# Top-k attention and a low-rank mixer on one core: first batch searched without folding and masked by GpSimd, second batch masked by the gap on both heads

## The chip, the cores and the metric

The kernel runs on one core of a Trainium2 chip. The metric is the device time of one execution in microseconds, as the median of several runs. The engines are PE (TensorE, matmuls), ACT (ScalarE), DVE (VectorE), POOL (GpSimd) and SP (SyncE, which issues the transfers here). Each works through its own stream of instructions in a fixed order; semaphores make one wait for another.

## The reference

Attention keeps, in each row of scores, the 32 largest, and then a block mixes over the sequence and over the channels. Everything is float32.

```python
B, H, S, D = q.shape                      # 8, 8, 576, 64
scores = scale * np.matmul(q, k.transpose(0, 1, 3, 2))
kth = np.partition(scores, -top_k, axis=-1)[..., -top_k:-top_k + 1]   # top_k = 32
mask = scores >= kth
scores = np.where(mask, scores, -1000000000.0)
attn = softmax(scores); attn_out = np.matmul(attn, v)
x = attn_out.transpose(0, 2, 1, 3).reshape(B, S, H * D)               # 8, 576, 512
h = x.transpose(0, 2, 1) @ U @ V                                      # rank 32
u = x + h.transpose(0, 2, 1)
out = u + np.maximum(u @ w_ch1, 0.0) @ w_ch2                          # 512 -> 2048 -> 512
```

(The softmax is written out in the original: the maximum is subtracted, and 1e-9 is added to the sum.)

## The kernel before

**Tiles and steps.** The 8 batches of 8 heads are 32 groups `g` of two heads (`NP`), four groups (`NPAIR`) a batch. The 576 query rows of a group are cut into four chunks of 128 rows with both heads (`t` = 0 to 3) and a last one (`t` = `NT` = 4), in which the remaining 64 rows of both heads share the 128 partitions. A pair (g, t) is a step `n = 5 g + t`; there are 160. Steps 0 to 19 are the first batch (`ALONE` = 20), 20 to 39 the second. From step 30 on (`ROUNDED`), for t below 4, `shared(g, t)` is true: there DVE and transfers turn the weights round rather than PE.

**One step.** `scores` makes S2, the tile Ssb of 128 x 2 x 576 scores, with PE and ACT copies. `front` searches each row's 32nd largest value with DVE: four times MAX8 (eight largest), with MATCH_REPLACE8 between them. It is a generator, advanced at several places of the main loop, and so spreads a step's work over its own and the following step.

**Folding.** Where a step has an entry in `folds`, each row's halves of 288 are folded: `pair` adds the halves as integers on POOL (L370, stage 0), takes their maximum on DVE (L372) and subtracts it from the sum on POOL (L373, stage 1), which leaves the smaller of each two. DVE searches the lower half with two MAX8 and one MATCH_REPLACE8 of 288 (L412, L414, L416), adds the 16 values found to the upper half, and does the four rounds on 304 elements instead of 576 (L426, L438, L443). Before, every step but (0, 0) is folded. `lower` has one buffer.

**Masking.** `ways(g, t)` says which heads are masked how. An "early" head gets its exponential on ACT within the search (L377, into a tile E), and DVE multiplies it by the mask and sums it (L446). A "gap" head gets, at the beginning of the next step, a very large number wherever a score lies below the 32nd (L461 and L464 on ACT), which POOL subtracts (L467), and then the exponential on ACT, which also sums (L377). Before, a two-head step outside `shared` masks head 1 early and head 0 by the gap; a shared one masks both by the gap and gives the exponential of head 1 a yield of its own (`ahead`). (3, 3) and (3, 4), the end of the first batch, have rules of their own.

**The rest.** `turns` transposes the weights with PE (L522, L527) and copies them with ACT (L523, L528); `values` multiplies by v (L556, L560, L546); `mixed` applies the low-rank mixer (L581 to L614); `mlp` is the large matmul part (L629, L648), which `fill` feeds in small portions as filler between the steps, by a fixed account (`share`, `due`). The filler begins when the first batch's attention is done. `next_params` loads the mixer's and the large part's weights and converts them: three ACT passes (L174, L175, L178), a shift on DVE (L186) and two integer additions on POOL (L187, L189), called a join below; this goes on until 326 us.

**Order.** The order on each engine is that in which the Python code issues instructions. In the first batch a step n runs: first MAX8 of step n; gap of step n - 1; scores and fold part one of n + 1; `values` of n - 3 and the `turns` of n - 2; second round of n; a join at t below 3; third round; exponential of n - 1; fold part two of n + 1; fourth round; a join at t = 0, 1 and 3; masking product of n. The first step whose DVE instructions come in a group is therefore L412, or L426 where nothing is folded.

Of the kernel before, what the change touches and what calls it, by code (L numbers as in the profile page):

```python
# [8 lines left out]
F32 = mybir.dt.float32  # L9
# [3 lines left out]
ALU = mybir.AluOpType  # L13

TOPK = 32
NEG = -3.0e38
# [10 lines left out]
def kernel(  # L27
# [28 lines left out]
    nc = tc.nc  # L56
    B, H, S, D = q.shape
    P = 128
# [4 lines left out]
    NT, TAIL = 4, 64  # L63
# [3 lines left out]
    NPAIR = H // 2  # L67
    NP = B * NPAIR

    CH = NT + 1  # L70
    ALONE = NPAIR * CH
# [11 lines left out]
    attn = ctx.enter_context(tc.tile_pool(name="attn", bufs=2))  # L83
# [265 lines left out]

    def fold(g, t):  # L350

        if 0 < g + t and g < NP:
            upper = attn.tile([P, 2, HALF + TOPK // 2], F32, tag="upper", name="upper")
            lower = attn.tile([P, 2, HALF], F32, tag="lower", name="lower", bufs=1)
            folds[g, t] = upper, lower
            pair(g, t, 0)
# [6 lines left out]
    def pair(g, t, stage):  # L363
        S2 = S2s[g, t]
        n = S2.shape[1]
        upper, lower = folds[g, t]
        top, bottom = upper[:, 0:n, 0:HALF], lower[:, 0:n].bitcast(U32)
        a, b = S2[:, :, 0:HALF], S2[:, :, HALF:S]
        if stage == 0:
            nc.gpsimd.tensor_tensor(bottom, a.bitcast(U32), b.bitcast(U32), ALU.add)  # L370
        else:
            nc.vector.tensor_tensor(top, a, b, ALU.max)  # L372
            nc.gpsimd.tensor_tensor(bottom, bottom, top.bitcast(U32), ALU.subtract)  # L373

    def weigh(chunk, E, nmax, total=None):

        nc.scalar.activation(E, chunk, AF.Exp, bias=nmax, scale=SCALE, accum_out=total)  # L377

    def ways(g, t):

        if (g, t) == (NPAIR - 1, NT - 1):
            return (0,), (1,)
        if (g, t) == (NPAIR - 1, NT):
            return (0,), ()
        if t == NT:
            return (), (0,)
        return ((), (1, 0)) if shared(g, t) else ((1,), (0,))

    def eased(g, t):
        return bool(ways(g, t)[1])  # L390

    def front(g, t):

        if t == 0:
            dens[g] = small.tile([P, 2 * NT + 1], F32, tag="den", name="den", bufs=3)
        S2, den = S2s.pop((g, t)), dens[g]
        n = S2.shape[1]  # L400
        chunks = [S2[:, c] for c in range(n)]
        sums = [den[:, 2 * t + c : 2 * t + c + 1] for c in range(n)]
        first = small.tile([P, 2, 8], F32, tag="first", name="first", bufs=3)
        nmax = small.tile([P, 2], F32, tag="nmax", name="nmax", bufs=4)
        order = (1, 0) if n == 2 else (0,)
        folded = (g, t) in folds
        if folded:
            upper, lower = folds.pop((g, t))
            curs = [upper[:, c] for c in range(n)]
            spots = [[upper[:, c, HALF + i : HALF + i + 8] for c in range(n)] for i in (0, 8)]  # L410
            for c in order:
                nc.vector.max(spots[0][c], lower[:, c])  # L412
            for c in order:
                nc.vector.match_replace(lower[:, c], spots[0][c], lower[:, c], NEG)  # L414
            for c in order:
                nc.vector.max(spots[1][c], lower[:, c])  # L416
        else:
            curs = list(chunks)
            places = [
                mlpp.tile([P, 2, WIDE], F32, tag="hT", name="hT", bufs=HT)  # L420
                .rearrange("p c n -> p (c n)")[:, 0:S]
                for _ in range(n)
            ]
        ms = [first[:, c] for c in range(n)]
        for c in order:
            nc.vector.max(ms[c], curs[c])  # L426
        yield
        early, gaps = ways(g, t)
        for i in range(1, TOPK // 8):
            if i == 1:  # L430
                nc.scalar.mul(nmax[:, 0:n], first[:, 0:n, 0], -SCALE)
                Es = {c: attn.tile([P, S], F32, tag="E", name="E") for c in early}
                for c in early:
                    weigh(chunks[c], Es[c], nmax[:, c : c + 1])
            for c in order:

                nxt = places[c] if i == 1 and not folded else curs[c]
                nc.vector.match_replace(nxt, ms[c], curs[c], NEG)  # L438
                curs[c] = nxt
            m8 = small.tile([P, 2, 8], F32, tag="m8", name="m8", bufs=4)  # L440
            ms = [m8[:, c] for c in range(n)]
            for c in order:
                nc.vector.max(ms[c], curs[c])  # L443
            yield
        for c in early:
            nc.vector.scalar_tensor_tensor(  # L446
                out=chunks[c],
                in0=chunks[c],
                scalar=ms[c][:, 7:8],
                in1=Es[c],  # L450
                op0=ALU.is_ge,
                op1=ALU.mult,
                accum_out=sums[c],
            )
        if t == NT:
            del qkTs[g]
        yield
        if gaps:
            lo, hi = min(gaps), max(gaps) + 1
            least = small.tile([P, 2], F32, tag="least", name="least", bufs=3)  # L460
            nc.scalar.mul(least[:, lo:hi], m8[:, lo:hi, 7], WIDEN)  # L461
            for c in gaps:
                gap = attn.tile([P, S], F32, tag="E", name="E")
                nc.scalar.activation(  # L464
                    gap, chunks[c], AF.Relu, bias=least[:, c : c + 1], scale=-WIDEN
                )
                nc.gpsimd.tensor_tensor(chunks[c], chunks[c], gap, ALU.subtract)  # L467
            yield
        ahead = order[0:1] if shared(g, t) else ()
        for c in ahead:  # L470
            weigh(chunks[c], chunks[c], nmax[:, c : c + 1], sums[c])
            yield
        for c in order:
            if c not in early and c not in ahead:
                weigh(chunks[c], chunks[c], nmax[:, c : c + 1], sums[c])
        if t == NT and g != NPAIR - 1:
            nc.scalar.activation(den, den, AF.Identity, bias=eps)
        yield

    def shared(g, t):  # L480


        return t < NT and g * CH + t >= ROUNDED
# [237 lines left out]
    def fill(k=1):  # L721


        nonlocal due
        for _ in range(k):
            if passes:
                passes.pop(0)()
            if mixing and next(mixing[0], True):
                mixing.pop(0)
            due += share * (SHORT if t == NT else 1) * (EARLY if n <= 2 * ALONE + 2 else 1)  # L730
            while due > 0:
                if not fillers:
                    due = 0.0
                    break
                done = next(fillers[0], None)
                if done is None:
                    fillers.pop(0)
                else:
                    due -= done
# [3 lines left out]
    t = 0  # L743
# [5 lines left out]
    for n in range(STEPS + 2):  # L749
        g, t = divmod(n, CH)  # L750
        if n < STEPS:
            if t == 0 and g + 1 < NP:
                load(g + 1)
            if t == 1 and g + 1 < NP:
                ready = prep(g + 1)
            fronts[n] = front(g, t)
            next(fronts[n])
        here, last = fronts.get(n, iter(())), fronts.pop(n - 1, iter(()))
        if n >= ALONE - 1 and n <= ALONE:

            if n < ALONE:
                next(last)
                values(*divmod(n - 3, CH))
                list(turning)
                next(here)
                next(last)
                scores(*divmod(n + 1, CH))
                fold(*divmod(n + 1, CH))
                values(*divmod(n - 2, CH))
# [11 lines left out]
            fill()  # L781
            scores(*divmod(n + 1, CH))
            fold(*divmod(n + 1, CH))
            next(here)
            while mixing:
# [9 lines left out]
            fill()  # L795
            continue
        ease = eased(*divmod(n - 1, CH))
        if n < ALONE:
            if ease:
# [26 lines left out]
        away = n <= STEPS and shared(*divmod(n - 1, CH))  # L826
# [6 lines left out]
        next(turning, None)  # L833
        fill()
        next(turning, None)
        if away:
            next(last)
        fill()
        next(turning, None)
        fill()  # L840
# [55 lines left out]
```

## Time and profile before

| | |
|---|---|
| median of 3 runs | 1759.32 us (1758.77 to 1759.58) |
| the profiled execution | 1761.93 us, of which the span of the profile is 1760.2 us |
| busy: PE, DVE, ACT, POOL | 1641.2, 1528.0, 1025.6, 965.7 us |
| fold, POOL L370 and L373 | x159 each, 218.3 and 204.3 us |
| gap subtraction, POOL L467, 128x576 | x263, mean 1410 ns |
| masking product, DVE L446, 128x576 | x25, 768 to 1668 ns, median 805 |
| maximum of a fold, DVE L372 | x159, mean 899 ns |
| MAX8 of 304 elements (L443) | x858, mean 464 ns |
| MAX8 and MATCH_REPLACE8 of 576 elements, first step | mean 744 and 740 ns |
| gap, ACT L464, 128x576 | x263, mean 769 ns |

A row of a timeline gives the start, the time, the engine, the line, the operation, output and inputs, and in brackets the idle time ahead of it with what ended it. Successive instructions of an engine overlap a little, so the distance from start to start is what one costs in a queue that is never empty: two paired MAX8 of 304 elements show 0.84 us together and start a new instruction 0.76 us later. Times of POOL rows are rougher than others.

### The profile page before, as it was taken

What the parts mean: (1) busy time and instruction counts of PE and PEld (TensorE: products, weight loads), DVE (VectorE), ACT (ScalarE), POOL (GpSimd) and SP (SyncE); (2) the same over time, 40 slices, a digit from 0 to 9 for tenths busy, and PEclk for the clock granted to TensorE, in tenths of its full rate; (3) what the DMA queues carried; (4) which work ended last, traced back from release to release, by engine and by line L of the source; (5) the groups of instructions that cost most, each with busy time, mean ns of one, the idle gap of its engine ahead of it and who ended that gap; (6) DMA issues with size and microseconds to landing.
All of it is one profiled execution on the core that took longest, in us unless ns stands there. A gap on an engine that the chain in (4) does not pass through costs nothing.

```text
span 1760.2 us, 29931 instructions
## 1 busy us (share of the span) xinstructions
PE 1641.2 (93%) x9435; PEld 1205.2 (68%) x9435; DVE 1528.0 (87%) x4559; ACT 1025.6 (58%) x2659; POOL 965.7 (55%) x759
## 2 busy tenths in 40 slices
PE   4566698999999999999999999999999999999999
PEld 2344465777667776677767776677767876678677
DVE  7999899999999999999999999999999999994000
ACT  5676777665655656565565665665666656563100
POOL 4776757655655555655555565655556555652000
PEclk7787789999999999999999999999999999999999
DMA  3222213144444443444444444444444444432010
GB/s 95 82 69 81 69 61 93 37 113 114 119 103 117 100 118 103 120 106 110 121 111 106 108 117 106 113 113 106 117 114 112 110 113 110 113 92 81 4 16 12
DMA packets 275838, 167.37 MB, mean 95 GB/s; under 512 B 173920, under 2 KB 260192, under 8 KB 275680
## 3 DMA queue, kind: packets, MB, share of 16 engines
q1 hardware_dynamic: 274624, 165.20, 36.2%
q8 instruction: 74, 1.21, 0.3%
q14 instruction: 84, 0.69, 0.1%
q10 hardware_dynamic: 1056, 0.26, 0.1%
HBM read 101.42 MB, written 63.96 MB: 94 GB/s over the span
## 4 chain that ended last, share of the span: by engine, by line
PE 70%; DVE 17%; DMA 3%; POOL 3%; issue 2%; SPq 2%; ACT 2%; POOLq 0%; DVEq 0%; ACTq 0%
PE mm L648 25%; PE mm L629 23%; PE sc L335 6%; PE O L560 6%; DVE upper L438 4%; DVE m L443 3%; DMA PT<-away 2%; DVE upper L372 2%; PE O L546 2%; DVE lower L414 2%; PE sc L323 2%; DVE first L426 1%; PE up L604 1%; PE tp L527 1%; DVE upper L412 1%
## 5 line engine op out<-in xcount | busy, mean ns | idle before, releaser
L648 PE MATMUL mm<-hT,w 128*128 128x256 f32 (+1 forms) x2048 | 545.8, 411 | 0.5 <-ACT hT L641 0.5
L629 PE MATMUL mm<-uT,w 128*128 128x256 f32 (+1 forms) x2048 | 539.9, 411 | 0.0
L467 POOL TENSOR_TENSOR Ssb<-Ssb,E 128x576 f32<-128x576 f32 x263 | 366.5, 1410 | 266.5 <-ACT E L464 265.9
L629 PEld LDWEIGHTS mm<-uT,w 128*128 128x128 f32 x2048 | 376.0, 192 | 99.9 <-issue 13.5
L648 PEld LDWEIGHTS mm<-hT,w 128*128 128x128 f32 x2048 | 374.5, 192 | 95.2 <-issue 11.5
L443 DVE MAX8 m<-upper 128x8 f32<-128x304 f32 x858 | 367.0, 464 | 3.3
L373 POOL TENSOR_TENSOR lower<-lower,upper 128x576 uint32<-128x576 uint32 (+1 forms) x159 | 204.3, 1285 | 163.2 <-DVE upper L372 153.1
L370 POOL TENSOR_TENSOR lower<-Ssb 128x576 uint32<-128x576 uint32 (+1 forms) x159 | 218.3, 1373 | 79.7 <-ACT Ssb L348 27.5
L438 DVE MATCH_REPLACE8 upper<-m,upper 128x304 f32<-128x304 f32 x572 | 257.9, 457 | 0.0
L641 ACT ACTIVATE hT<-mm 128x320 f32<-128x320 f32 (+1 forms) x256 | 105.7, 413 | 202.1 <-PE mm L629 200.3
L377 ACT ACTIVATE Ssb<-Ssb,nmax 128x576 f32<-128x576 f32 x263 | 204.7, 783 | 3.1 <-POOL Ssb L467 3.1
L464 ACT ACTIVATE E<-Ssb,least 128x576 f32<-128x576 f32 x263 | 192.5, 769 | 5.2
L335 PE MATMUL sc<-qkT 64*128 64x288 f32 x1024 | 169.9, 452 | 10.3 <-ACT Ssb L346 8.8
L412 DVE MAX8 upper<-lower 128x8 f32<-128x288 f32 x286 | 116.9, 445 | 46.2 <-POOL lower L373 46.2
L560 PE MATMUL O<-PT,va 128*64 128x128 f32 x2048 | 145.0, 285 | 8.4 <-DMA PT<-away 8.2
L372 DVE TENSOR_TENSOR upper<-Ssb 128x576 f32<-128x576 f32 (+1 forms) x159 | 142.9, 899 | 11.2 <-ACT Ssb L348 10.6
L494 DVE STREAM_TRANSPOSE y<-Ssb 128x512 f32<-128x512 f32 x208 | 138.4, 692 | 7.5 <-ACT Ssb L377 6.6
L335 PEld LDWEIGHTS sc<-qkT 64*128 64x128 f32 x1024 | 92.5, 196 | 73.9 <-issue 29.0
L560 PEld LDWEIGHTS O<-PT,va 128*64 128x64 f32 x2048 | 113.5, 141 | 25.7 <-DMA PT<-away 11.1
L438 DVE MATCH_REPLACE8 upper<-first,upper 128x304 f32<-128x304 f32 x286 | 129.3, 458 | 0.0
L661 DVE TENSOR_TENSOR oT<-uT,mm 128x320 f32<-128x320 f32 (+1 forms) x8 | 3.6, 454 | 140.8 <-PE mm L648 140.8
L414 DVE MATCH_REPLACE8 lower<-upper,lower 128x288 f32<-128x288 f32 x286 | 124.6, 442 | 0.0
(93 smaller groups left out, 1979.4 us busy)
## 6 DMA issues: line engine op xcount, KB each, us to landing
away<-y SPq DMA_DIRECT2D x416, 128.0 KB, 2.4
PT<-away SPq DMA_DIRECT2D x104, 512.0 KB, 3.3
raw<-in_moe_w_ch_dram SPq DMA_DIRECT2D x32, 512.0 KB, 3.8
va<-in_v_dram SPq DMA_DIRECT2D x64, 128.0 KB, 2.3
out_dram<-ob SPq DMA_DIRECT2D x57, 128.0 KB, 2.0
ld<-in_q_dram SPq DMA_DIRECT2D x108, 64.0 KB, 2.6
ld<-in_k_dram SPq DMA_DIRECT2D x108, 64.0 KB, 2.3
ld<-in_q_dram SPq DMA_DIRECT2D x108, 8.0 KB, 2.2
```

The source lines that it names most:

```text
L335: nc.tensor.matmul(sc[:, h, 0:HALF], lhsT=qkT[half(h), 0, cols(t)], rhs=qkT[half(h), 1, i * HALF : (i + 1) * HALF], start=True, stop=True,)
L370: nc.gpsimd.tensor_tensor(bottom, a.bitcast(U32), b.bitcast(U32), ALU.add)
L372: nc.vector.tensor_tensor(top, a, b, ALU.max)
L373: nc.gpsimd.tensor_tensor(bottom, bottom, top.bitcast(U32), ALU.subtract)
L377: nc.scalar.activation(E, chunk, AF.Exp, bias=nmax, scale=SCALE, accum_out=total)
L438: nc.vector.match_replace(nxt, ms[c], curs[c], NEG)
L443: nc.vector.max(ms[c], curs[c])
L464: nc.scalar.activation(gap, chunks[c], AF.Relu, bias=least[:, c : c + 1], scale=-WIDEN)
L467: nc.gpsimd.tensor_tensor(chunks[c], chunks[c], gap, ALU.subtract)
L560: nc.tensor.matmul(O[half(h)], lhsT=va[:, h, j, :], rhs=PB[:, h, j] if shared(g, t) else PT[:, NT * h + j], start=False, stop=(j == NT - 1),)
L629: nc.tensor.matmul(ph[:, 0:w], lhsT=w1[:, cc, f * P : (f + 1) * P], rhs=uT[:, cc, lo:hi], start=(cc == 0), stop=(cc == NC - 1),)
L648: nc.tensor.matmul(po[:, 0:w], lhsT=w2[:, f, c * P : (c + 1) * P], rhs=hTs[f][:, 0:w], start=(f == 0), stop=(f == NF - 1),)
```

## The change

The fold is confined to groups 4 to 31; all of the first batch is searched on 576 elements. `ways` returns three tuples now: early, pooled and gap heads. Groups 0 to 3, for t below 4, mask head 1 by the new way "pooled": at the end of the search POOL compares the scores with the 32nd value and multiplies by -3e38 (one instruction with two operations), then adds the result to the scores; the exponential follows in the next step with that of head 0, which keeps the gap. The rules for (3, 3) and (3, 4) stay. Groups 4 to 31 mask both heads by the gap, which for groups 4 and 5 is new. `ahead` and the place of a `next(last)` in the main loop follow the number of gap heads, no longer `shared`.

```diff
     def fold(g, t):
-        if 0 < g + t and g < NP:
+        if NPAIR <= g < NP:
...
     def ways(g, t):
         if (g, t) == (NPAIR - 1, NT - 1):
-            return (0,), (1,)
+            return (0,), (), (1,)
         if (g, t) == (NPAIR - 1, NT):
-            return (0,), ()
+            return (0,), (), ()
         if t == NT:
-            return (), (0,)
-        return ((), (1, 0)) if shared(g, t) else ((1,), (0,))
+            return (), (), (0,)
+        return ((), (1,), (0,)) if g < NPAIR else ((), (), (1, 0))
     def eased(g, t):
-        return bool(ways(g, t)[1])
+        return bool(ways(g, t)[2])
...
-        early, gaps = ways(g, t)
+        early, pooled, gaps = ways(g, t)
...
             yield
+        for c in pooled:
+            gap = attn.tile([P, S], F32, tag="E", name="E")
+            nc.gpsimd.tensor_scalar(gap, chunks[c], ms[c][:, 7:8], NEG, ALU.is_lt, ALU.mult)
+            nc.gpsimd.tensor_tensor(chunks[c], chunks[c], gap, ALU.add)
         for c in early:
...
-        ahead = order[0:1] if shared(g, t) else ()
+        ahead = order[0:1] if len(gaps) == 2 else ()
...
         next(turning, None)
-        if away:
-            next(last)
+        if n > ALONE and (n - 1) % CH < NT:
+            next(last, None)
         fill()
```

The stream of instructions on PE is the same before and after. In the program of the changed kernel POOL's stream in the first batch reads, for a two-head step, the comparison (128x576), the addition, and in the next step the gap subtraction, with the joins of the weights between.

## The prediction

> **What bounds the kernel now.** I read the two busy rows of the page, then busy time by stage, then the order of time on VectorE (DVE) and GpSimd (POOL) in those stages. The first batch (pair groups 0 to 3) ends at about 210 us; the stages below are cut where the first DVE instruction of a group starts. Columns: stage, its length, busy time (count) of PE, PEld, DVE, ACT, POOL, granted clock, DMA share, GB/s.
>
> ```profile
> PE   4566698999999999999999999999999999999999
> DVE  7999899999999999999999999999999999994000
> ...
> 0.00:58.70 58.70, 31.78 (x159) 19.53 (x159) 48.44 (x141) 32.51 (x77) 30.75 (x42) 0.74 0.37 96
> 58.70:111.77 53.07, 30.87 (x196) 20.67 (x196) 49.62 (x146) 38.70 (x89) 38.60 (x28) 0.77 0.27 78
> 111.77:164.90 53.13, 32.91 (x193) 21.83 (x193) 49.68 (x147) 38.78 (x89) 38.60 (x28) 0.75 0.27 77
> 164.90:210.44 45.54, 24.62 (x160) 16.61 (x159) 42.99 (x132) 33.87 (x77) 31.94 (x24) 0.77 0.22 64
> 234.84:279.37 44.53, 39.24 (x208) 26.72 (x207) 41.31 (x115) 34.14 (x77) 32.54 (x25) 0.92 0.26 78
> 440.00:1580.00 1140.00, 1134.51 (x6669) 834.00 (x6668) 1090.42 (x3282) 695.06 (x1864) 662.30 (x513) 1.00 0.43 111
> ```
>
> See: in the first batch PE works 31 of 53 us and DVE nearly all; from 440 us on PE has 5 us idle in 1140. PE's instruction stream is the same before and after, so a microsecond gained ahead of the filled stretch should reach the end. DVE's gaps and swollen rows there come from POOL:
>
> ```profile
> 65.38 1.78 DVE L372 TENSOR_TENSOR upper<-Ssb 128x576 f32<-128x576 f32 x1
> 76.98 0.73 DVE L372 TENSOR_TENSOR upper<-Ssb 128x576 f32<-128x576 f32 x1
> 90.64 1.64 DVE L446 SCALAR_TENSOR_TENSOR Ssb<-Ssb,m,E 128x576 f32<-128x576 f32 x1
> 94.83 0.82 DVE L412 MAX8 upper<-lower 128x8 f32<-128x288 f32 x2 [2.55 <-POOL lower L373]
> ...
> 93.38 1.41 POOL L373 TENSOR_TENSOR lower<-lower,upper 128x576 uint32<-128x576 uint32 x1
> ```
>
> The fold's maximum takes 0.73 or 1.78 us, the masking product 0.80 or 1.64, and the next step waited 2.55 us for the fold's second half. In the second batch PE waits on ACT's chain of copies:
>
> ```profile
> 271.68 0.33 PE L527 MATMUL tp<-ident,Ssb 128*128 128x128 f32 x1 [1.75 <-ACT PT L523]
> ...
> 268.35 0.20 ACT L461 ACTIVATE least<-m 128x1 f32<-128x1 f32 x1 [1.40 <-DVE m L443]
> 268.59 0.78 ACT L464 ACTIVATE E<-Ssb,least 128x576 f32<-128x576 f32 x1
> ```
>
> One step of the new kind is already in the trace, the very first, which isn't folded:
>
> ```profile
> 10.92 1.42 DVE L426 MAX8 first<-Ssb 128x8 f32<-128x576 f32 x2 [0.93 <-ACT Ssb L348]
> 12.32 0.74 DVE L438 MATCH_REPLACE8 hT<-first,Ssb 128x576 f32<-128x576 f32 x1
> 21.25 0.20 DVE L186 TENSOR_SCALAR uT<-uT 128x128 uint32<-128x128 uint32 x1
> ```
>
> **What the Trainium skill says.** "SBUF — State Buffer", section "Who interferes with whom": DVE instructions with two SBUF inputs, or in a two-port mode, and GpSimd instructions that read SBUF exclude each other for a whole instruction; a DVE instruction with one input outside those modes doesn't contend. The trace agrees: L372 and L446 double, L186 goes from 0.40 to 1.22, while MAX8 and MATCH_REPLACE8 never move. "GPSIMD Engine Reference", section "Engine selection": one-input work is "roughly line-rate" there, two-input work about half of DVE's speed. The trace has no large one-input POOL row; its 128x576 two-input row is 1.41 us.
>
> **The change, part by part.**
>
> *A. First batch, rows not folded.* 19 steps lose three 288-wide passes a head, L372 on DVE and both fold instructions on POOL; the other seven passes a head grow from 304 to 576. From the first step: 10.92 to 21.25 is 10.33 us, less the 0.66 that its L372 occupied, gives 9.67 us for a two-head step. For a folded one, pairs start every 0.73, 0.79, 0.72, 0.75, then three of 0.88 and three of 0.76: 7.9 us, plus L372 at 0.7 to 1.75. So the search itself costs about 1.0 us more, and with L372 and its stalls gone it is near even. One-head steps (t = 4): the single 304 passes start 0.13 us farther apart than the paired ones, so 576 wide I take 0.80 a MAX8 and 0.86 a replace: 4 x 0.80 + 3 x 0.86 = 5.8.
>
> *B. First batch, second head masked by POOL.* 15 L446 leave DVE (0.74 start to start, 1.6 when blocked; 16 L446 took 15.4 us in 10.9 to 210.44, and (3, 3) and (3, 4) keep theirs). POOL gets 15 comparisons and 15 additions of 128x576. Addition: 1.41. Comparison: not in the trace. Below: line rate, 576 elements at 1.2 GHz, 0.5 us (an estimate from that page). Above: the same page's section "Elementwise — side-by-side cycle accounting" gives data-dependent branching about 12 cycles an element, 5.8 us plus start, say 6.0 (estimate). I take 0.9, between line rate and the two-input row. In place of two fold instructions of 1.41 POOL is then no busier than before. The second exponential moves on ACT from inside its step to the next one, behind the POOL addition; instructions on ACT stay as many.
>
> *Who waits for POOL then?* Not DVE: its passes need only score copies, issued a whole step ahead. In the step with most POOL work (t = 1) the queue from the step's start is: rest of the weight joins 2.7, comparison 0.9, addition 1.4, gap subtraction 1.4: 6.4 us, and ACT's exponentials end about 7.3 us into a step of over 10. The transposes that read them are issued a step later. So this is covered; the cover is gone when the comparison takes above about 3.5 us. L186 can still be blocked; its six in a group took 0.32, 0.32, 0.83, 1.14, 0.73 and 0.33 from start to start, 3.7, and I keep that.
>
> Sum for groups 1 and 2: 4 x 9.67 + 5.8 + 3.7 + 0.1 (reciprocal) = 48.3 against 53.07 and 53.13: -4.8 each. Group 0 (10.92 to 58.70 is 47.8): 38.7 + 5.8 + 1.3 of joins = 45.8: -2.0. Group 3's first four steps (45.54): 38.7 + 3.7 + 0.1 + 0.74 = 43.2: -2.3. Together -13.9.
>
> *C. The hand-over (3, 4).* Step (4, 0) is folded as before, inside (3, 4), and its L372 waits 2.91 us for score copies behind POOL and ACT, a chain that stays. After it come two replace/maximum rounds: 3.3 us at 576 against 2.05 now: +1.3.
>
> *D. Second batch (groups 4 and 5), both heads by the gap.* Eight L446 leave DVE: 8 x 0.74 = -5.9 at most. Added: eight gaps on ACT (0.68 start to start) and eight subtractions on POOL (1.41), both before the next fold; the exponential again moves. POOL's queue holds, in order: both subtractions, fold part one, a join, fold part two, at t = 1 and 3 another join. Following it from the rows: DVE already waited 2.54, 2.98 and 1.16 us for L373 at 234.84, 279.37 and 332.61. (4, 1) starts unchanged, since its L373 came last already. For (4, 3), POOL runs join 246.70 to 249.8, one subtraction, L370, join, and L373 from 256.27 to 257.68; with a second gap of 0.68 on ACT ahead of the pass (L178) that this join waits for, and a second subtraction of 1.41, L373 ends about 259.5, where DVE would now be ready at 257.0 and before was at 258.49: I put the step 0.5 to 1.0 late instead of 1.5 early. (5, 0), where POOL was already last, adds 1.4: about 1.9 late; (5, 1) gets 0.74 back: 1.15. The second gap also stands ahead of the copies that PE waits for at 271.68 and 303.69 (0.7). At 303.69, after which the chain is PE's: 1.15 + 0.7 = +1.9. I take that; bounds -5.9 (POOL never last) and +11.3 (all eight subtractions in line).
>
> *E. Position of `next(last)`.* It only runs the extra yield that D creates; no cost of its own. SP's queue is not moved.
>
> Sum: -13.9 + 1.3 + 1.9 = -10.7. The profiled span 1760.2 (1761.9 with what lies around it) becomes 1749.5; the runs' median lies 2.6 below that execution, so 1759.3 - 10.7 = 1748.6.
>
> **The rivals.**
> 1. *The second batch gains too.* POOL finds gaps enough (it is busy 32.5 of 44.5 us there) and D gives -4 to -6: -12.6 - 5.9 = -18.5, 1741. Against: the waits for L373 already there.
> 2. *POOL takes L373's place fully in D*: every subtraction in line, -12.6 + 11.3 = -1.3, 1758, within what can be measured. Against: at (5, 1) and (5, 2) POOL waited for DVE, not the reverse.
> 3. *Slower: POOL becomes the bound in the first batch by its comparison.* At 6.0 us a group of five steps asks POOL for 4 x (6.0 + 1.41 + 1.41) + 1.41 + 6 joins x 2.9 + 1.1 = 55.2 against 53.1 now: groups 1 and 2 +2.1 each, group 0, which has smaller joins, stays on DVE (-2.0), group 3 about +0.8, then +1.3 and +1.9: +6.2, 1765.5. It decides from about 5.5 us a comparison. For it: no row shows the instruction; against it: line rate for one input.
> 4. *The change doesn't do what it says*: the port's exclusion returns on L186 or ACT holds up score copies, eating half of A and B: 1755.
>
> **How the numbers follow.** Chances: forecast 0.57 (own range 1744 to 1754), rival 1 0.15, rival 2 0.12, rival 3 0.08, rival 4 0.08. The range 1739 to 1758 takes in 1, 2 and 4 and leaves out 3 and the ends of 1. A measurement of this kernel tells 0.2% (3.5 us) from no change, so faster is below 1755.8: forecast, rival 1, half of 4, a little of 2: 0.80; same 0.10; slower 0.10.
>
> **What would show it.** Right: no L412 before (4, 0); first-batch DVE without gaps, groups near 48 us; comparison about 0.9 us; (3, 4) starting near 197 us; PE's waits at (4, x) and (5, x) somewhat longer. Wrong: ACT or POOL as releaser of L426 in the first batch, POOL near full, or L373 waits over 1.5 us at most steps of groups 4 and 5.

## The result, and the profile after

The changed kernel takes 1746.65 us (median; 1743.84 to 1747.74), the kernel before, on the same chip, 1759.45 (1758.77 to 1761.39). The ratio is 0.9923, with a 95% interval of 0.9906 to 0.994: 12.8 us faster. The two profiled executions lie farther apart, 1761.93 and 1745.95 us (spans 1760.2 and 1744.1), one above its median and the other below, so sums made in the profile come out at 16, not 12.8. Lines of the changed kernel behind 445 have numbers four higher than before: L446 is now L450, L467 is L471, L523 is L527.

Busy time by stage of the changed kernel, cut at the same places as before: the first DVE instruction of groups 1, 2 and 3, of step (3, 4), of (4, 1), of (5, 0) and of (6, 0). Columns: stage, length, busy time (count) of PE, PEld, DVE, ACT, POOL, granted clock, DMA share, GB/s.

```profile
0.00:57.15 57.15, 29.95 (x155) 18.58 (x155) 47.21 (x100) 30.40 (x75) 28.31 (x39) 0.73 0.36 97
57.15:103.91 46.76, 29.38 (x179) 19.75 (x180) 46.48 (x98) 37.92 (x91) 37.99 (x27) 0.74 0.26 75
103.91:150.68 46.77, 32.19 (x214) 21.59 (x214) 46.49 (x98) 39.51 (x95) 38.00 (x27) 0.82 0.31 91
150.68:192.50 41.82, 26.64 (x155) 18.23 (x153) 41.82 (x89) 33.89 (x81) 33.21 (x24) 0.71 0.25 78
192.50:215.99 23.49, 18.63 (x131) 13.06 (x133) 17.38 (x49) 17.09 (x41) 14.26 (x11) 1.00 0.28 62
215.99:260.98 44.99, 40.09 (x206) 26.20 (x203) 39.51 (x109) 37.07 (x86) 37.54 (x29) 0.92 0.29 79
260.98:316.72 55.74, 51.07 (x285) 34.70 (x285) 50.35 (x140) 39.89 (x95) 44.48 (x35) 0.94 0.23 58
```

DVE is busy 46.5 of 46.8 us in groups 1 and 2. Against before (my subtraction, us; group 0 from DVE's first MAX8 on):

| stage | before | after | difference |
|---|---|---|---|
| start up to the first MAX8 | 10.92 | 11.23 | +0.3 |
| group 0 | 47.78 | 45.92 | -1.9 |
| group 1 | 53.07 | 46.76 | -6.3 |
| group 2 | 53.13 | 46.77 | -6.4 |
| group 3 without (3, 4) | 45.54 | 41.82 | -3.7 |
| (3, 4) and (4, 0) | 24.40 | 23.49 | -0.9 |
| (4, 1) to (5, 4) | 97.77 | 100.73 | +3.0 |
| from (6, 0) to the end | 1427.59 | 1427.38 | -0.2 |

In the profile the first batch gives 18 us, and the stretch (4, 1) to (5, 4) takes 3 back. What DVE waits for in the first batch (11 to 192 us), in the view of waits: engine, what, total, times, longest:

```profile
DVE first L426 <- ACT Ssb L348: 0.9, 1, 0.9
```

That one wait is at the very start. POOL's new comparison, in the view of its line (shortest, median and longest in ns, first and last start), and a step's POOL rows in the timeline:

```profile
L447 POOL TENSOR_SCALAR E<-Ssb,m x15: 2207/2217/2253, 22.2 to 183.3; 128x576 f32<-128x576 f32 x15
...
180.66 1.31 POOL L187 TENSOR_TENSOR w<-w,raw 128x512 uint32<-128x512 uint32 x1
182.05 1.29 POOL L189 TENSOR_TENSOR w<-w,raw 128x512 uint32<-128x512 uint32 x1
183.31 2.21 POOL L447 TENSOR_SCALAR E<-Ssb,m 128x576 f32<-128x576 f32 x1
185.61 1.41 POOL L448 TENSOR_TENSOR Ssb<-Ssb,E 128x576 f32<-128x576 f32 x1
186.97 1.41 POOL L471 TENSOR_TENSOR Ssb<-Ssb,E 128x576 f32<-128x576 f32 x1
```

The comparison takes 2.21 us, more than the two-input addition of the same size with its 1.41. In the second batch, the waits for the fold at (5, 0) and (6, 0) have grown (DVE timeline; they were 2.98 and 1.16):

```profile
260.98 0.82 DVE L412 MAX8 upper<-lower 128x8 f32<-128x288 f32 x2 [4.35 <-POOL lower L373]
316.72 0.82 DVE L412 MAX8 upper<-lower 128x8 f32<-128x288 f32 x2 [3.89 <-POOL lower L373]
```

### The profile page after: what moved, and what is told of

Same layout as the page of the kernel before. It is cut to its first block, busy times and chain, and to the rows that moved or that the text cites. A ratio compares the mean times of both kernels' runs of the same rounds, so it can differ in the third digit from the quotient of the medians.

```text
span 1744.1 us, 29711 instructions
## 1 busy us (share of the span) xinstructions
PE 1638.1 (94%) x9435; PEld 1202.4 (69%) x9435; DVE 1515.5 (87%) x4358; ACT 1030.4 (59%) x2690; POOL 973.2 (56%) x759
## 4 chain that ended last, share of the span: by engine, by line
PE 73%; DVE 16%; ACT 3%; DMA 3%; POOL 3%; issue 2%; SPq 1%; POOLq 0%; DVEq 0%; ACTq 0%
PE mm L652 26%; PE mm L633 23%; PE sc L335 6%; PE O L564 6%; DVE m L443 5%; DVE hT L438 3%; DVE upper L438 2%; DMA PT<-away 2%; PE sc L323 2%; DVE first L426 2%; PE O L550 2%; PE up L608 1%; PE tp L531 1%; PE O L560 1%; PE tp L526 1%
## 5 line engine op out<-in xcount | busy, mean ns | idle before, releaser
L471 POOL TENSOR_TENSOR Ssb<-Ssb,E 128x576 f32<-128x576 f32 x271 | 379.4, 1418 | 270.5 <-ACT E L468 269.9
L443 DVE MAX8 m<-upper 128x8 f32<-128x304 f32 x756 | 323.9, 466 | 2.9
L373 POOL TENSOR_TENSOR lower<-lower,upper 128x576 uint32<-128x576 uint32 (+1 forms) x140 | 180.5, 1289 | 137.2 <-DVE upper L372 130.5
L377 ACT ACTIVATE Ssb<-Ssb,nmax 128x576 f32<-128x576 f32 x286 | 222.6, 783 | 17.2 <-POOL Ssb L448 9.2
L370 POOL TENSOR_TENSOR lower<-Ssb 128x576 uint32<-128x576 uint32 (+1 forms) x140 | 194.8, 1392 | 59.3 <-DVE first L426 18.3
L438 DVE MATCH_REPLACE8 upper<-m,upper 128x304 f32<-128x304 f32 x504 | 227.6, 459 | 0.0
L412 DVE MAX8 upper<-lower 128x8 f32<-128x288 f32 x252 | 103.0, 445 | 41.0 <-POOL lower L373 41.0
L372 DVE TENSOR_TENSOR upper<-Ssb 128x576 f32<-128x576 f32 (+1 forms) x140 | 123.7, 884 | 11.6 <-ACT Ssb L348 11.0
L346 ACT COPY Ssb<-sc 128x576 f32<-128x576 f32 x127 | 80.6, 635 | 71.4 <-PE sc L335 69.9
L573 ACT COPY XT<-O 128x128 f32<-128x128 f32 x128 | 34.2, 267 | 143.1 <-PE O L564 143.1
```

## The experiments

My theory: DVE's own work sets the first batch once it waits for nobody, so both parts there count in full and together; the second batch's part costs a little, through POOL's queue ahead of the fold. Line numbers shift with the edits: in experiment 1, and in the last kernel of experiment 4, `ways` is two lines longer (L412 becomes L414, L373 stays); a repeated comparison moves what stands behind L447 by one or two.

**1. Each part alone.** Four kernels on one chip, before at 1759.97 us. The first keeps only the first batch's part, the second only the second batch's. The third unfolds the first batch but masks its second head on DVE; the fourth folds it and masks its second head on POOL; in both, groups 4 and 5 stay as before. The first as a diff against the changed kernel; the third differs from it in the first returned tuple, `((1,), (), (0,))`, and the fourth in having the old condition of `fold`. The second has both of these and keeps the changed kernel's last two lines and its rule for groups 4 and 5.

```diff
-        return ((), (1,), (0,)) if g < NPAIR else ((), (), (1, 0))
+        if g < NPAIR:
+            return ((), (1,), (0,))
+        return ((), (), (1, 0)) if shared(g, t) else ((1,), (), (0,))
...
-        if n > ALONE and (n - 1) % CH < NT:
-            next(last, None)
+        if away:
+            next(last)
```

> First batch changed (not folded, second head masked by POOL), groups 4 and 5 masked as before. Theory: the whole gain is DVE's shorter steps in the first batch, and the second batch's part costs 1.9 us; so about 1.9 us faster than the changed kernel, 1744.7, with the (3, 4) step starting near 192.5 us and (4, 1) to (6, 0) taking 97.8 us as in the kernel before. Rival (the second batch's part gains, through eight masking products less on DVE): slower than the changed kernel by 3 to 6 us, 1750 to 1753.

> First batch as before, groups 4 and 5 with both heads masked by the gap. Theory: 1.9 us slower than the kernel before, about 1761.3, with L412 waiting for L373 more than the 7.3 us of before in 234 to 460 us. Rival (second batch gains): 1754 to 1756.

> First batch not folded, but the second head still masked on DVE by L446. Theory (DVE's own work sets the first batch once it no longer waits for the fold): each of 15 steps is 0.74 to 0.8 us longer than in the changed kernel, so (3, 4) starts 11 to 12 us later, near 204 us, and the time is about 1754, 5 to 6 us faster than before. Rival (the fold's stalls on POOL were nearly all of it, and L446 without the fold beside it costs nothing on the path): within 2 us of the run with only the first batch changed. Other rival (unfolding gains nothing by itself because it makes DVE's search longer): 1759.

> First batch still folded, second head masked by POOL. Theory (the two parts need each other): POOL gets 2.2 and 1.4 us a step on top of the two fold instructions, 38.6 + 4 x 3.6 = 53 us a group, as much as the group took, and DVE waits for L373 at nearly every step: 3 to 10 us slower than before, 1762 to 1769. Rival (parts add up, taking L446 off DVE gives 15 x 0.74 = 11 us whatever the fold does): 1748.

| kernel | median, us | ratio to before (95%) |
|---|---|---|
| first batch only | 1743.91 | 0.991 (0.9897 to 0.9924) |
| second batch only | 1764.24 | 1.0023 (1.0012 to 1.0033) |
| unfolded only | 1752.24 | 0.9958 (0.9945 to 0.997) |
| masked by POOL only | 1780.33 | 1.0115 (1.01 to 1.013) |

The first batch's part is worth 16.1 us and the second batch's costs 4.3 by itself. Their sum, -11.8, is the change's -12.8 within the scatter. In the first kernel (4, 1) to (5, 4) takes 97.77 us, exactly as before. In the second, whose cost I had put at 1.9 us, that stretch takes longer (before: 97.77 us, POOL 71.84, DVE 93.12 of it):

```profile
233.62:335.71 102.09, 92.30 (x489) 62.01 (x487) 89.54 (x248) 76.87 (x180) 82.52 (x63) 0.92 0.24 67
```

DVE has 3.6 us less work there, POOL 10.7 more, and the stretch is 4.3 us longer: the products taken off DVE were replaced by waiting. From there to 460 us DVE waits 13.0 us for L373, against 7.3 before. That a part makes DVE's row smaller says nothing of its worth where DVE then waits.

Unfolding alone gives 7.7 us. DVE is again never idle after the start, and a group is 49.2 us:

```profile
60.13:109.34 49.21, 30.64 (x195) 20.20 (x192) 49.00 (x106) 38.66 (x88) 24.93 (x18) 0.77 0.29 83
```

Against group 1 before (53.07 us, DVE busy 49.62) that is 3.9 us less, of which 3.2 is idle time of DVE that is gone and only 0.6 its work: unfolding pays by the waits it ends, not by a shorter search. Step (3, 4) starts at 202.15 us against 192.36 in the first kernel, with POOL masking added: 9.8 us for 15 products, 0.65 each where I had put 0.74 to 0.8. The difference is about what DVE loses again on L186, which takes 0.41 us in the mean here (11 to 190 us) and 0.48 with POOL masking.

Masking on POOL without unfolding costs 20.4 us, where I had expected 3 to 10, and the parts are far from adding up: -7.7 and +20.4 against -16.1 together. Group 1 of that kernel as a stage, its waits, and rows of its POOL timeline:

```profile
64.32:122.69 58.37, 31.04 (x196) 20.65 (x196) 46.02 (x139) 39.10 (x94) 51.46 (x37) 0.74 0.24 71
```

```profile
DVE upper L414 <- POOL lower L373: 17.0, 4, 4.9
```

```profile
91.12 2.21 POOL L449 TENSOR_SCALAR E<-Ssb,m 128x576 f32<-128x576 f32 x1
93.41 1.62 POOL L450 TENSOR_TENSOR Ssb<-Ssb,E 128x576 f32<-128x576 f32 x1
94.98 1.42 POOL L473 TENSOR_TENSOR Ssb<-Ssb,E 128x576 f32<-128x576 f32 x1
96.34 1.94 POOL L370 TENSOR_TENSOR lower<-Ssb 128x576 uint32<-128x576 uint32 x1
98.24 1.04 POOL L592 TENSOR_TENSOR x<-x,den 128x512 f32<-128x512 f32 x1
99.24 1.29 POOL L187 TENSOR_TENSOR w<-w,raw 128x512 uint32<-128x512 uint32 x1
100.61 1.28 POOL L189 TENSOR_TENSOR w<-w,raw 128x512 uint32<-128x512 uint32 x1
101.86 1.39 POOL L373 TENSOR_TENSOR lower<-lower,upper 128x576 uint32<-128x576 uint32 x1
```

POOL isn't even full (51.5 of 58.4 us). The masking of the step just ended stands ahead of the fold that the next step starts with, and DVE waits for it up to 4.9 us a step. My sum took POOL's load for the measure; the rows and waits say that it is the place in the queue. No run keeps the load and moves the masking behind the fold, so this is read from the trace and not shown by an edit.

**2. How much room POOL has in the first batch.** The comparison issued twice (the diff), and three times:

```diff
             nc.gpsimd.tensor_scalar(gap, chunks[c], ms[c][:, 7:8], NEG, ALU.is_lt, ALU.mult)
+            nc.gpsimd.tensor_scalar(gap, chunks[c], ms[c][:, 7:8], NEG, ALU.is_lt, ALU.mult)
```

> The changed kernel with POOL's comparison issued twice (same result): 2.2 us more of POOL in each of 15 steps of the first batch. Theory (in the first batch DVE waits for nobody; POOL has room): the queue of the fullest step grows from 7.7 to 9.9 us and ACT's exponentials end about 10.8 us after the start of a step of 10.3 to 10.8, so cover is just about used up: 0 to 3 us slower than the changed kernel, 1747 to 1750, groups 46.8 to 47.8 us. Rival (POOL is on the path there, and the comparison of 2.2 us instead of the 0.9 of the prediction was paid in full): 15 x 2.2 = 33 us slower, 1780.

> The changed kernel with the comparison issued three times: 6.6 us a step in place of 2.2. Theory: POOL now holds 4 x (6.7 + 2.8) + 1.4 + 6 x 2.7 + 1.1 = 56.7 us of work a group and sets the group: about 10 us more in each of groups 1 and 2, 5 to 8 in groups 0 and 3, so 25 to 35 us slower than the changed kernel, 1772 to 1782. Rival (POOL stays off the path): under 5 us slower.

Measured, with before at 1757.98: twice 1764.56 us, ratio 1.0035 (1.0023 to 1.0048); three times 1797.63, ratio 1.0227 (1.0212 to 1.0243). Against the changed kernel's ratio of 0.9923 the second comparison costs about 20 us of the 33 that full price would be (15 times 2.2), and the third its 33. Both expectations were wrong: 0 to 3 us for one more, and 25 to 35 for two more, which cost 53. What ACT waits for, in the kernel with two comparisons (11 to 205 us; in the changed kernel 9.2 us in 7 waits), what DVE waits for, a DVE row just ahead of (3, 4), and what POOL waits for in groups 1 and 2 (56.63 to 159.75 us):

```profile
ACT Ssb L377 <- POOL Ssb L449: 25.5, 12, 4.9
```

```profile
DVE first L426 <- ACT Ssb L348: 5.2, 3, 2.4
DVE w L186 <- ACT w L174: 2.9, 2, 1.4
DVE m L443 <- POOL E L448: 0.8, 1, 0.8
```

```profile
207.54 0.90 DVE L451 SCALAR_TENSOR_TENSOR Ssb<-Ssb,m,E 128x576 f32<-128x576 f32 x1 [3.64 <-ACT E L377]
...
POOL w L187 <- ACT raw L178: 4.6, 2, 2.3
POOL Ssb L472 <- ACT E L469: 3.8, 2, 1.9
```

I had looked at one step's queue, which still ended in time. Over a group POOL has 38.0 us of work, and four more comparisons at 2.3 from start to start make 47.2, a little more than the 46.8 that DVE needs. That alone would cost 0.4 us a group. But POOL also waits for ACT, 4.2 us a group (half of the 8.4 above; the same waits are 4.1 in the changed kernel): 51.4 together, and groups 1 and 2 take 50.15 and 52.97, 51.6 in the mean. So POOL's order of work, with its waits in it, sets the group. With three comparisons the same sum gives 60.6, and group 1 takes 61.3 (DVE's first MAX8 at 61.63 and 122.93 us).

The lateness reaches DVE over ACT: exponentials that wait for POOL hold up the score copies and weight passes that stand behind them, and DVE waits for these. The first batch is 15.9 us longer ((3, 4) starts at 208.37 us, not 192.50): 8.0 of new waits in the view above, 3.6 at the row of (3, 3), and 4.0 by L186, which takes 0.71 us in the mean (11 to 190 us) instead of 0.48. Another 3.0 us comes after the first batch.

**3. Downward, and by which way lateness reaches DVE.** In the first kernel both heads of the first batch are masked by the gap, so the 2.21 us comparison and the 1.41 us addition become one subtraction and an ACT instruction. In the second, the kernel with two comparisons gets eight result buffers in place of four, because DVE waits 0.8 us for one that a comparison still reads.

```diff
-        return ((), (1,), (0,)) if g < NPAIR else ((), (), (1, 0))
+        return ((), (), (1, 0))
...
-        ahead = order[0:1] if len(gaps) == 2 else ()
+        ahead = order[0:1] if len(gaps) == 2 and g >= NPAIR else ()
```

```diff
-            m8 = small.tile([P, 2, 8], F32, tag="m8", name="m8", bufs=4)
+            m8 = small.tile([P, 2, 8], F32, tag="m8", name="m8", bufs=8)
```

> The changed kernel with both heads of the first batch masked by the gap: POOL's comparison (2.2 us) and addition (1.4) become one subtraction (1.4), ACT gets one more gap (0.7) in each of 15 steps. Theory (in the changed kernel DVE waits for neither POOL nor ACT in the first batch, so neither load matters in the downward direction): within 1.5 us of the changed kernel, 1745 to 1748, groups of 46.7 us again. Rival (the comparison of 2.2 us costs something already): 3 to 6 us faster than the changed kernel, 1741 to 1744.

> The kernel with the comparison issued twice, and eight buffers in place of four for the eight-value results (m8) that the late comparison still holds when DVE wants to write the next. Theory (POOL's lateness reaches DVE mainly over ACT: exponentials that wait for POOL stand ahead of the score copies and weight passes that DVE needs): 0 to 3 us of the 18 are gained, 1761 to 1765. Rival (it reaches DVE through the held result buffers): 8 us or more gained, below 1756.

Measured, with before at 1758.68: 1746.72 us, ratio 0.9929 (0.9917 to 0.9942), the changed kernel's time; and 1764.1, ratio 1.003 (1.002 to 1.0039), no gain over two comparisons with four buffers. So the single comparison costs nothing that shows, and with two the way to DVE is ACT's queue and not the held buffers: with eight of them that wait is gone and the time stays. With three comparisons the held buffers count too; there DVE's largest wait is for them (11 to 205 us, 18.7 of 35.8 us in all):

```profile
DVE m L443 <- POOL E L449: 18.7, 7, 3.9
```

**4. A version that beats both.** If the second batch suffers from the fold behind POOL's other work, it should not be folded either while the weights are being joined. Fold from group 6 on; the search's scratch goes into the fold's idle buffers, which the large matmul part doesn't use:

```diff
-        if NPAIR <= g < NP:
+        if NPAIR + 2 <= g < NP:
...
             places = [
-                mlpp.tile([P, 2, WIDE], F32, tag="hT", name="hT", bufs=HT)
+                attn.tile([P, 2, HALF + TOPK // 2], F32, tag="upper", name="upper")
                 .rearrange("p c n -> p (c n)")[:, 0:S]
```

> The changed kernel with groups 4 and 5 not folded either (fold from group 6 on; the search's scratch in the fold's own buffers), both heads by the gap. Theory (in groups 4 and 5 DVE waits for the fold behind the weight joins on POOL, and PE behind that): no L373 waits before 320 us, the hand-over (3, 4) is 3 us shorter since no fold stands in it, and PE waits less; faster than the run with only the first batch changed, 1737 to 1742. Rival (PE's filled stream bounds groups 4 and 5 already): 1743 to 1746.

> As the run with groups 4 and 5 not folded, but their head 1 masked on DVE (L446) as in the kernel before. Theory: DVE gets 0.74 us a step back on its load and POOL and ACT lose 1.4 and 0.7; between the other runs, 1738 to 1743. If masking by the gap is what helps where nothing is folded, it is 2 to 5 us slower than the run above; if not, within 2 us of it.

Measured, with before at 1757.98: 1732.42 us, ratio 0.9857 (0.9843 to 0.987), and with head 1 masked on DVE in groups 4 and 5 1732.96, ratio 0.9858 (0.9845 to 0.9872). Both are better than expected (1737 to 1742 and 1738 to 1743), 25 us faster than before. DVE rows of the former, at the hand-over, and what PE waits for between 192 and 330 us:

```profile
192.18 0.75 DVE L426 MAX8 first<-Ssb 128x8 f32<-128x576 f32 x1
198.18 0.77 DVE L450 SCALAR_TENSOR_TENSOR Ssb<-Ssb,m,E 128x576 f32<-128x576 f32 x1
198.87 1.42 DVE L426 MAX8 first<-Ssb 128x8 f32<-128x576 f32 x2
```

```profile
PE O L560 <- ACT PT L532: 2.2, 4, 0.7
PE tp L531 <- ACT PT L527: 1.9, 2, 1.0
PE tp L526 <- ACT XT L573: 1.6, 2, 1.0
PE pT L596 <- ACT PT L527: 1.6, 1, 1.6
```

(3, 4) takes 6.7 us, from 192.18 to 198.87, where it took 10.9 with the fold of (4, 0) inside it. By stages of the profile, against the changed kernel, (3, 4) and (4, 0) give 5.9 us (17.56 in place of 23.49) and (4, 1) to (5, 4) 6.6 (94.16 in place of 100.73). L531 waits 1.9 us in all for the copy L527, against 4.7 in the changed kernel, and L596 1.6 in place of 3.2. Gap and product masking come out equal here, so with no fold behind it the gap on both heads costs nothing. This points to the fold as what made it dear in the change.

## Why the prediction was right

- *Direction and size*: forecast -10.7 us, measured -12.8, inside the range. In the profile the sum is -16.1: the first batch gives 4.4 us more than forecast, the hand-over 2.2 more, and the stretch (4, 1) to (5, 4) takes 1.1 more. Set beside the medians, the forecast looks closer than its terms are.
- *A and B, the first batch*: the mechanism held: DVE idle nowhere after the start, and the part alone gives the gain. The size was forecast as 48.3 us a group and is 46.76. A two-head step without joins is 9.65 (9.67 forecast), the one-head step 5.69 (5.8). The mis-sized term is the six L186: I kept 3.7 us from the trace before, and they take 2.4. In group 1 only one of the six is stretched, to 0.85 us, by a POOL addition that began before it; the others take 0.41, and two of these run in the middle of POOL's comparison (rows in the last section). Over groups 1 to 3 that makes 1.4 to 1.5 us each.
- *B, the comparison*: forecast 0.9 us, measured 2.21, so the price was wrong by a factor of 2.5. The forecast didn't suffer because POOL had room for it, as experiment 3 shows. The limit of "about 3.5 us" for its cover is not contradicted: at 2.2 us the cover holds, at 4.4 it is gone, and no run lies between. But the rival's "about 5.5 us a comparison" for slower than before was too high: at 4.4 us the kernel is already 6.6 us slower than before.
- *C, the hand-over*: forecast +1.3, measured +0.5 for (3, 4) (10.38 to 10.87 us) and -1.4 for (4, 0), -0.9 together. The longer passes came as forecast, and in (3, 4) a small normalizing row of DVE that took 0.81 us takes 0.15, which I hadn't counted. Of the 1.4, 1.05 belongs to the second batch's part: with the first batch's alone the two steps take 24.54 us, with both 23.49. In (4, 0) there is then no L446 of 1.57 us beside POOL's first fold part, which goes from 1.93 to 1.41.
- *D, the second batch*: forecast +1.9. The sum is right in the profile and its make-up is not. Against the kernel with the first batch's part alone, (3, 4) and (4, 0) take 1.05 us less, where the forecast had no change, and (4, 1) to (5, 4) 2.96 more: +1.9. By itself the part costs 4.3 us. DVE's side is what the rows show: both subtractions stand ahead of the fold, and DVE waits 0.9, 4.35, 0.9 and 3.9 us at (4, 3), (5, 0), (5, 3) and (6, 0). PE's side failed. The forecast has PE 1.9 us late at its instruction of 303.69. In the changed kernel and in that with the first batch's part alone this instruction is:

```profile
285.77 1.03 PE L596 MATMUL pT<-x,U 128*32 128x128 f32 x10 [3.19 <-ACT PT L527]
...
285.74 0.60 PE L598 MATMUL pT<-x,U 128*32 128x128 f32 x10 [3.38 <-ACT PT L529]
```

  That is 17.92 and 17.95 us earlier than before: up to there the second batch has cost PE nothing. From there to the end of the span the changed kernel loses 1.8 us against before, and it lies in the next 54 us. The same stretch of PE's stream before, with the first batch's part alone, changed, with the second batch's part alone, and with three comparisons:

```profile
303.69:356.25 52.56, 52.37 (x307) 36.24 (x308) 51.13 (x153) 34.65 (x87) 37.84 (x31) 0.97 0.22 54
285.74:338.30 52.56, 52.37 (x307) 36.29 (x308) 51.12 (x153) 34.69 (x87) 37.87 (x31) 0.97 0.23 54
285.77:340.27 54.50, 53.82 (x307) 36.64 (x307) 49.11 (x144) 36.16 (x93) 41.04 (x33) 0.95 0.22 52
303.47:359.26 55.79, 53.95 (x306) 36.91 (x307) 49.68 (x144) 36.16 (x93) 41.32 (x33) 0.94 0.20 45
338.07:391.49 53.42, 52.71 (x307) 35.85 (x307) 48.04 (x144) 36.06 (x93) 41.06 (x33) 0.97 0.22 53
```

  In the four kernels without the second batch's part it takes 52.5 to 52.6 us at a granted clock of 0.97. With it, over the fold, it takes 54.5 to 56.1 at 0.94 or 0.95 in five kernels, and 53.4 at 0.97 in the one with three comparisons; not folded, 51.7 and 50.9 at 1.00. So the loss that the forecast gave to late copies goes here for the most part with a lower clock. What lowers the clock is open. That the total met the +1.9 is luck.
- *The rivals*: that the second batch gains is refuted by the kernel with its part alone, 4.3 us slower, and the kernel without it is not slower than the changed one. That POOL takes the fold's place fully there is too much: 3 us, not 11. That POOL bounds the first batch is what happens with a second comparison.

Not settled are what lowers that clock, and why the profiled executions lie 16.0 us apart and the medians 12.8.

## What to carry to other kernels

Where two engines hand work to and fro, price a moved instruction by what stands behind it in its queue: the same POOL masking costs 20 us with a fold behind it and gains 8 without. Two edits that look separable can be worth little or less than nothing each and much together, so run the parts. Check cover over a whole period and not over its fullest step, and count the engine's own waits in it: 47.2 us of work and 4.2 of waiting made 51.4 here, in a period of 46.8.

## What the runs showed of the hardware that was not expected

POOL's one-input instruction with two operations and a scalar per partition, a comparison and a multiplication on 128x576 float32, takes 2.21 us; its two-input addition of that size takes 1.41. The prediction, leaning on the Trainium skill's "GPSIMD Engine Reference", section "Engine selection", had taken one-input work to be the cheaper; here the measurement decides. This is one form and one size; other one-input forms were not run.

The exclusion of DVE and POOL, which the prediction cites and finds in the rows of before, does not show for this comparison. Two pairs of the changed kernel's group 1 (POOL's addition and comparison, each with the shift that starts within it):

```profile
76.70 1.30 POOL L189 TENSOR_TENSOR w<-w,raw 128x512 uint32<-128x512 uint32 x1
77.44 0.85 DVE L186 TENSOR_SCALAR w<-w 128x512 uint32<-128x512 uint32 x1
...
81.05 2.25 POOL L447 TENSOR_SCALAR E<-Ssb,m 128x576 f32<-128x576 f32 x1
82.38 0.40 DVE L186 TENSOR_SCALAR w<-w 128x512 uint32<-128x512 uint32 x1
```

In all six meetings of this second kind in the changed kernel (groups 1 to 3, the shift starting 1.2 to 1.3 us after the comparison) L186 takes 0.40 to 0.42 us and the comparison 2.21 to 2.25. In the kernel of experiment 1 that folds and masks on POOL, the fold's maximum L372 takes 0.74 us in the three such meetings. Where the measurement differs from what the prediction cites, it decides; earlier phases of the comparison were not met in this way.
